# A retention-plus-hard-swish kernel: W_in loaded in eight equal pieces, six short zero matmuls at the begin, one load of the sixth GEMM2 issued later

## The chip, the cores and the metric

One core of a Trainium2 chip runs the whole program. The metric is device time in microseconds of one execution. The kernel before took 286.35 us, the median of three runs (286.25 to 286.49). Engines in the profile: PE (TensorE matmul), PEld (its weight load), DVE (VectorE), ACT (ScalarE), POOL (GpSimd, which issues nearly all loads here), SP (SyncE, which issues stores and transposing DMAs).

## The reference

Two stages, one after the other, on fp32 inputs:

```python
# q, k, v: (8 batches, 8 heads, 576 positions, 64)
scores = q @ k.T / sqrt(64)
ret    = scores * D            # D[i, j] = gamma_h ** (i - j) for i >= j, else 0
x      = (ret @ v)             # heads side by side: (4608 tokens, 512)
h      = x @ w_in              # (4608, 2048)
g      = h * clip(h + 3, 0, 6) / 6
out    = g @ w_out             # (4608, 512), float32
```

## The kernel before

The attention is computed in pieces of 128 positions. A piece turns its own scores against the lower triangle and adds what a running 64 x 64 state per head carries over from the pieces before (linear attention in chunks). The pieces of eight batches are taken in the order of position, so that four pieces fill one block of 512 tokens; there are nine blocks. The 64 positions that are left in each batch form four "rest" pieces, numbers 32 to 35, and the last block.

For each block, GEMM1 multiplies the block's x (512 channels, transposed) with W_in in 16 units of four matmuls of 512 columns (line 478); ACT and DVE make the hard-swish from the PSUM result (lines 486 and 487). GEMM2 multiplies the 2048 features with W_out. For the first two blocks this is 64 plain matmuls of 512 columns (line 541). From the third block on it is `g2_seven`: seven half-size products in the manner of Strassen, 14 units of eight matmuls of 256 columns (line 627), with sums of the weights and of the tokens made ahead on DVE. PE goes through the blocks in a fixed order written out by hand: GEMM1 of a block, GEMM2 of it, GEMM1 of the next. Between units, lists such as `steps_at`, `load_in_gemm2` and `load_in_gemm1` put in the other work: attention steps on PE (`step4`, lines 389, 411, 439 and 357: 128 matmuls of 64 x 64 in all), multiplications and transposing DMAs of the coming piece (`ahead`), and loads (`load_next`).

How the work around the change is ordered:

- **Start.** Batches come in pairs. The first pairs' q, k and v are loaded by `first_load`, converted to fp16, turned by PE (line 262), and give the first block's x. While the first data is on its way, PE multiplies zeros (`warm`, line 226). Weights are then loaded by POOL in the order of lines 690 to 702: W_in in six pieces, three quarters of W_out, pair 2 of q, k, v, the last quarter of W_out, pair 3.
- **First GEMM1.** It begins with three pairs of half-block products (line 506) from the first columns of W_in, and goes on in units of 128 columns: f = 4, 5, ... to 15. W_in's first four loads cover 256 of the 2048 columns each (f = 0,1; 2,3; 4,5; 6,7), the last two 512 each (f = 8 to 11; 12 to 15).
- **POOL's queue.** POOL issues DMAs in program order, and a DMA waits until the eighth one before it has landed, since there are eight semaphores for them.
- **Later loads.** `load_next` issues one third of a piece (k, then q, then v), after the newest matmul that PE has been given at that place in the lists (`newest[0]`, line 759). A rest piece's third is two DMAs.

```python
load_in_gemm2 = {kb: ... (0, 2, 4, 6, 8, 10, 12) ...}    # after which units a third is loaded
load_in_gemm2[5] = (0, 2, 4, 6, 11, 12, 13)              # block 5: the sixth GEMM2
```

Of the kernel before, what the change touches and what calls it, by code (L numbers as in the profile page):

```python
# [10 lines left out]
FP32 = mybir.dt.float32  # L11
# [6 lines left out]
def kernel(  # L18
# [16 lines left out]
    nc = tc.nc  # L35
# [3 lines left out]
    P = 128  # L39
# [4 lines left out]
    MBLK = 512  # L44
# [39 lines left out]
    def bank(shape, dtype, name):  # L84
        return psum.tile(shape, dtype, tag="ph", bufs=4, name=name)

    def bank_or(tag, shape, dtype, name):
        return psum.tile(shape, dtype, tag=tag, name=name) if tag else bank(shape, dtype, name)
# [40 lines left out]
    def load_win(f0, f1):  # L129
        return nc.gpsimd.dma_start(  # L130
            win16[:, :, f0:f1],
            moe_w_in.rearrange("(cc p) f -> p cc f", p=P)[:, :, f0:f1])
# [16 lines left out]
    zeros = const.tile([P, MBLK // 2], FP32)  # L149
# [69 lines left out]
    warmed = [0]  # L219

    def warm(n, tag=None):

        w = bank_or(tag, [P, 2, MBLK // 2], FP32, f"warm_{warmed[0]}")
        warmed[0] += 1
        for _ in range(n):
            nc.tensor.matmul(w, zeros[:, 0:P], zeros[:, None, :].to_broadcast([P, 2, MBLK // 2]),
                             start=True, stop=True)

    warm(3)

    def make_mask64():
        nc.vector.tensor_copy(mask64[0:HALF], mask01[0:HALF, 0:HALF])
# [455 lines left out]


    WQ = DFF // 4  # L690
    for i in range(4):
        load_win(i * (WQ // 2), (i + 1) * (WQ // 2))
    for i in range(2, 4):
        load_win(i * WQ, i * WQ + WQ)
    for i in range(3):
        load_wout(4 * i, 4 * i + 4)
    first_load(2, 0)
# [171 lines left out]
    for kb in range(1, NMB - 1):  # L869
        for at in {1: ((6, 6), (13, 13)), NMB - 2: ((6, 9),)}.get(kb, ((1, 3), (9, 11))):  # L870
            if groups[2:]:
                put_step(kb, at, groups[0], groups[1])
            else:
# [5 lines left out]
    load_in_gemm2 = {kb: (0, 2, 5, 7, 10, 12) if kb == 2  # L879
                     else (0, 2, 4, 8, 9, 11, 13) if kb == 3 else (0, 2, 4, 6, 8, 10, 12)  # L880
                     for kb in range(2, NMB - 3)}
    load_in_gemm2[1] = (2, 4, 8, 9, 12, 14)
    load_in_gemm2[5] = (0, 2, 4, 6, 11, 12, 13)
    load_in_gemm1 = {kb: (0, 2, 4, 7, 10, 13) for kb in range(2, NMB - 2)}
    load_in_gemm1[2] = (0, 1, 2, 4, 7, 10, 13)
    for kb in range(1, NMB):
# [52 lines left out]
```

## Time and profile before

| What | us |
|---|---|
| median of 3 runs | 286.35 |
| profiled execution, its own time | 285.78 |
| span of the profiled execution | 284.0 |
| PE busy | 275.5 (97%) |
| DVE busy | 229.2 (81%) |
| ACT busy | 171.2 (60%) |
| first GEMM1's units of 512 columns, first matmul | 18.05 |
| first GEMM2, first matmul | 28.9 |
| sixth GEMM2 | 182.4 to 197.4 |

The profiled execution lasts 1.78 us longer than its span and is 0.57 us below the median. The span is cut into busy time by engine; since PE is busy for 97% of it, the few places where PE has nothing to run are what is looked for. "idle before <-" names what ended an engine's idle time. A wait "<-issue" is one for which the profile shows no semaphore. The profile's DMA section splits the transfers by queue: "software_dynamic" holds what POOL issues, "hardware_dynamic" what SP and ACT issue, and "instruction" the engines' own programs, which are fetched by DMA too. A matmul's recorded time is longer than its distance from the next, since matmuls overlap: 512 columns are recorded with 379 ns and follow each other every 216 ns, 256 columns with 273 ns and every 109 ns.

### The profile page before, as it was taken

The page shows a single profiled execution, that of the slowest core. Times are in us where ns is not written, and L with a number is a line of the kernel's source. Part 1 is how long each engine was busy: PE and PEld are TensorE (multiplying, and loading weights), DVE is VectorE, ACT ScalarE, POOL GpSimd, SP SyncE. Part 2 cuts the span into 40 slices and gives each one's busy share as a digit, 9 for nine tenths or more (in the row PEclk, how much of TensorE's full clock was granted, in tenths as well). Part 3 has the DMA queues.
Part 4 walks back from the last instruction along what each step waited for, and adds up shares of the span by engine and source line. Part 5 has one row for each costly group of instructions (what it writes and reads, how often), then busy time and mean ns, then how long its engine had stood idle before and what let it go on. Part 6 is the DMA issues. An engine that isn't in the chain of part 4 may idle for free.

```text
span 284.0 us, 9017 instructions
## 1 busy us (share of the span) xinstructions
PE 275.5 (97%) x3824; PEld 180.0 (63%) x3824; DVE 229.2 (81%) x389; ACT 171.2 (60%) x296; POOL 103.2 (36%) x134
## 2 busy tenths in 40 slices
PE   7899999999999999999999999999999999999994
PEld 2564456875474786478646874597459745874583
DVE  6766765998889998999789978998899588727871
ACT  7778316872477637863676558755865487357710
POOL 8942578253353234324333344353750000000000
PEclk9999999999999999999999999999999999999999
DMA  9999999999999999997999999987992250121014
GB/s 136 186 201 206 190 182 178 213 141 142 184 130 160 142 95 151 165 116 77 145 178 125 95 132 167 150 86 111 152 188 50 76 111 0 42 78 36 0 39 111
DMA packets 144008, 35.98 MB, mean 127 GB/s; under 512 B 129728, under 2 KB 142912, under 8 KB 143968
## 3 DMA queue, kind: packets, MB, share of 16 engines
q0 software_dynamic: 104496, 18.23, 84.4%
q1 hardware_dynamic: 38496, 16.52, 29.2%
q10 hardware_dynamic: 976, 0.66, 0.8%
q8 instruction: 30, 0.49, 0.7%
q14 instruction: 10, 0.08, 0.1%
HBM read 36.70 MB, written 9.44 MB: 162 GB/s over the span
## 4 chain that ended last, share of the span: by engine, by line
PE 91%; DMA 4%; POOL 4%; issue 0%; DVE 0%; POOLq 0%
PE ph L478 36%; PE x L627 15%; PE pout L541 10%; PE z L627 9%; PE ph L506 6%; PE y L627 5%; DMA win<-in_moe_w_in_dram 4%; PE o L389 2%; PE o L411 2%; PE sc L357 2%; POOL qkn L121 2%; PE u L439 1%; PE xtu L627 1%; PE xo L627 1%; POOL win L130 1%; POOL vn L121 1%
## 5 line engine op out<-in xcount | busy, mean ns | idle before, releaser
L478 PE MATMUL ph<-xt,win 128*128 128x512 f16 x488 | 107.1, 379 | 0.3 <-DMA win<-in_moe_w_in_dram 0.3
L486 ACT ACTIVATE u<-ph,cb 128x512 f32<-128x512 f32 x122 | 83.5, 687 | 22.1 <-PE ph L478 22.0
L487 DVE SCALAR_TENSOR_TENSOR gt<-u,ph 128x512 f16<-128x512 f32 x122 | 81.2, 684 | 17.1 <-ACT u L486 15.9
L478 PEld LDWEIGHTS <-win 128*128 128x128 f16 x488 | 47.6, 98 | 56.1 <-DMA win<-in_moe_w_in_dram 0.8
L627 PEld LDWEIGHTS <-sum_s 128*128 128x128 f16 x448 | 43.3, 98 | 5.2
L107 POOL DMA_DIRECT2D qkn<-in_k_dram x32 | 26.6, 834 | 39.0 <-PE ph L478 11.0
L107 POOL DMA_DIRECT2D qkn<-in_q_dram x32 | 26.7, 839 | 29.0 <-PE ph L478 9.9
L107 POOL DMA_DIRECT2D vn<-in_v_dram x32 | 26.8, 838 | 26.6 <-PE ph L478 10.1
L627 PEld LDWEIGHTS <-gt 128*128 128x128 f16 x336 | 32.4, 98 | 5.7 <-issue 0.3
L541 PE MATMUL pout<-wout,gt 128*128 128x512 f16 x128 | 29.5, 380 | 0.0
L595 POOL DMA_DIRECT2D out_dram<-osb x1 | 0.6, 625 | 68.2 <-DVE osb L648 68.2
L627 PE MATMUL x<-wsum_t,sum_s 128*128 128x256 f16 x192 | 22.9, 273 | 0.0
L541 PEld LDWEIGHTS <-gt 128*128 128x128 f16 x128 | 11.8, 98 | 13.6
L506 PE MATMUL ph<-xt,win 128*128 128x256 f16 x176 | 20.1, 273 | 0.1
L344 DVE TENSOR_TENSOR qkn<-qkn,gqk 128x1024 f16<-128x1024 f16 x28 | 19.1, 684 | 0.0
L506 PEld LDWEIGHTS <-win 128*128 128x128 f16 x176 | 16.8, 98 | 2.9 <-DMA win<-in_moe_w_in_dram 0.4
L582 DVE TENSOR_TENSOR sum_s<-gt 128x1024 f16<-128x1024 f16 (+1 forms) x21 | 18.1, 863 | 0.2
L514 ACT ACTIVATE u<-ph,cb 128x512 f32<-128x512 f32 x22 | 15.0, 687 | 4.9 <-PE ph L506 4.7
L363 DVE TENSOR_TENSOR at<-sc,mask 128x1024 f16<-128x1024 f32 x14 | 17.0, 1216 | 1.1 <-PE sc L357 1.1
L515 DVE SCALAR_TENSOR_TENSOR gt<-u,ph 128x512 f16<-128x512 f32 x22 | 14.5, 683 | 2.8 <-ACT u L514 2.6
L423 ACT CAST xt<-o 64x512 f16<-64x512 f32 x28 | 16.2, 580 | 0.3
L421 ACT CAST xt<-o 128x512 f16<-128x512 f32 x14 | 8.2, 585 | 10.2 <-PE o L411 10.2
(112 smaller groups left out, 321.5 us busy)
## 6 DMA issues: line engine op xcount, KB each, us to landing
out_dram<-osb SPq DMA_DIRECT2D x24, 256.0 KB, 2.9
qkn<-in_k_dram POOLq DMA_DIRECT2D x32, 128.0 KB, 5.3
vn<-in_v_dram POOLq DMA_DIRECT2D x32, 128.0 KB, 5.0
qkn<-in_q_dram POOLq DMA_DIRECT2D x30, 128.0 KB, 5.3
out_dram<-osb SPq DMA_DIRECT2D x19, 128.0 KB, 5.0
wout<-in_moe_w_out_dram POOLq DMA_DIRECT2D x4, 512.0 KB, 14.9
win<-in_moe_w_in_dram POOLq DMA_DIRECT2D x4, 256.0 KB, 7.3
win<-in_moe_w_in_dram POOLq DMA_DIRECT2D x2, 512.0 KB, 11.4
```

The costliest lines, as they stand in the source:

```text
L107: loaded[c]["dma"].append(nc.gpsimd.dma_start(dst[p0:p0 + n], src[b, :, s0:s0 + n, :].rearrange("h s d -> s h d")))
L344: nc.vector.tensor_tensor(out=both, in0=both, in1=gqk, op=ALU.mult)
L363: nc.vector.tensor_tensor(out=at.rearrange("t a j p s -> t (a j p) s"), in0=sc.rearrange("t a j p s -> t (a j p) s"), in1=mask64[:, None, ...
L423: nc.scalar.copy(to[rows(h2), :, :, 1, :], o[1][rows(1 - h2)].rearrange("e j p s -> e p j s"))
L478: newest[0] = nc.tensor.matmul(ph, win16[:, dmc, P * fc:P * fc + P], xt_of(kb)[:, dmc, :], start=(dmc == 0), stop=(dmc == NCC - 1))
L486: nc.scalar.activation(u, ph, ACTF.Relu, bias=cb[:, 0:1], scale=1.0 / 6.0)
L487: nc.vector.scalar_tensor_tensor(out=gts[kb][:, fc, :], in0=u, scalar=1.0, in1=ph, op0=ALU.min, op1=ALU.mult)
L506: newest[0] = nc.tensor.matmul(ph[:, i], win16[:, dmc, P * (fc + i):P * (fc + i) + P], xt_of(kb)[:, dmc, cols], start=(i == 0 and dmc == 0 ...
L514: nc.scalar.activation(u, ph, ACTF.Relu, bias=cb[:, 0:1], scale=1.0 / 6.0)
L541: newest[0] = nc.tensor.matmul(pout, gt[:, fc, P * mc:P * mc + P], wout16[:, fc, :], start=(fc == 0), stop=(fc == NFC - 1))
L582: nc.vector.tensor_tensor(out=s(which)[:, c0:c1], in0=x(), in1=y(), op=op)
L627: newest[0] = nc.tensor.matmul(dst, left()[:, c, P * u:P * u + P], right[:, c, :], start=(first and c == 0 and (u == 0 or name not in whol ...
```

## The change

Three edits. W_in is loaded in eight pieces of 256 columns; its columns 1024 to 2047 came in two pieces of 512 and come in four. At the begin PE multiplies zeros six times with 256 columns, in place of three times with 512 columns (a view that showed the same 256 zeros twice); each of these fp32 matmuls stands in the trace as two weight loads' and two matmuls' records. In the sixth GEMM2 the fourth load, which is v of rest piece 32, is issued after unit 10 and not after unit 6.

```diff
     def warm(n, tag=None):
-        w = bank_or(tag, [P, 2, MBLK // 2], FP32, f"warm_{warmed[0]}")
+        w = bank_or(tag, [P, MBLK // 2], FP32, f"warm_{warmed[0]}")
         warmed[0] += 1
         for _ in range(n):
-            nc.tensor.matmul(w, zeros[:, 0:P], zeros[:, None, :].to_broadcast([P, 2, MBLK // 2]),
-                             start=True, stop=True)
-
-    warm(3)
+            nc.tensor.matmul(w, zeros[:, 0:P], zeros, start=True, stop=True)
+
+    warm(6)
...
     WQ = DFF // 4
-    for i in range(4):
+    for i in range(8):
         load_win(i * (WQ // 2), (i + 1) * (WQ // 2))
-    for i in range(2, 4):
-        load_win(i * WQ, i * WQ + WQ)
...
-    load_in_gemm2[5] = (0, 2, 4, 6, 11, 12, 13)
+    load_in_gemm2[5] = (0, 2, 4, 10, 11, 12, 13)
```

POOL issues two DMAs more; on every other engine the program's instructions are the same in the same order, apart from the zero matmuls.

## The prediction

> **What bounds the kernel now.** I read the page first: busy time, then the instruction queue.
>
> ```profile
> PE 275.5 (97%) x3824; PEld 180.0 (63%) x3824; DVE 229.2 (81%) x389; ACT 171.2 (60%) x296; POOL 103.2 (36%) x134
> ...
> q8 instruction: 30, 0.49, 0.7%
> ```
>
> PE is the bound, so only PE's idle time can go. PE's own program is also fetched by DMA: 30 packets, 0.49 MB, for 7648 matmuls and weight loads, so 64 bytes each and 256 instructions to a packet. Next the chain that ended last, in order of time:
>
> ```profile
> 8.48 2.89 POOL win L130 x4
> 11.37 10.59 DMA win<-in_moe_w_in_dram
> 22.00 7.08 PE ph L478 x32
> ...
> 135.09 0.67 issue
> ```
>
> The chain reaches PE at 22.00 through the load of W_in's third piece, and from there on it is nearly all PE. The timeline shows the wait, and the zeros at the begin:
>
> ```profile
> 1.19 0.50 PEld L226 LDWEIGHTS warm<-zeros 128*128 128x128 f32 x2 [1.19 <-DVE cb L153]
> 1.19 4.68 PE L226 MATMUL warm<-zeros 128*128 128x512 f32 x6 [1.19 <-DVE cb L153]
> 2.21 0.34 PEld L226 LDWEIGHTS warm<-zeros 128*128 128x128 f32 x1 [0.52 <-issue]
> ...
> 6.75 0.64 PE L262 MATMUL trq<-ident,qkn 128*64 128x128 f16 x16 [0.88 <-ACT qkn L181]
> ...
> 18.05 3.62 PE L478 MATMUL ph<-xt,win 128*128 128x512 f16 x16
> ...
> 22.00 7.08 PE L478 MATMUL ph<-xt,win 128*128 128x512 f16 x32 [0.33 <-DMA win<-in_moe_w_in_dram]
> ```
>
> Sixteen matmuls of 216 ns from 18.05 end their stream at 21.50; the next starts at 22.00. The wait is 0.50 us (the 0.33 is counted from the last one's recorded end). After it PE has no wait for a load. Three more places stop PE for no semaphore:
>
> ```profile
> 71.49 0.23 PEld L411 LDWEIGHTS <-vn 64*64 64x64 f16 x18 [0.16 <-issue]
> ```
> ```profile
> 135.75 0.25 PE L411 MATMUL o<-at,vn 64*64 64x64 f16 x7 [0.67 <-issue]
> ```
> ```profile
> 157.55 0.33 PEld L627 LDWEIGHTS <-gt 128*128 128x128 f16 x4 [0.30 <-issue]
> ```
>
> By the starts of neighbouring matmuls they cost 0.21, 0.83 and 0.19 us: 1.23 together. I counted PE's records: they stand at numbers 1985, 4033 and 4545, each 193 more than a multiple of 256. So PE stands there at the edge of a fetched packet. The packets before them are at 68.64 (1.28 long), 133.50 (0.93) and 154.49 (1.52); PE goes on 1.56, 1.33 and 1.55 after their ends.
>
> **The change, part by part.** *W_in in halves.* The issues and landings:
>
> ```profile
> win<-in_moe_w_in_dram POOLq DMA_DIRECT2D x1, 512.0 KB, 10.6
> win<-in_moe_w_in_dram POOLq DMA_DIRECT2D x1, 256.0 KB, 8.2
> ```
>
> The last 256-column piece was issued at 10.64 and landed at 18.84, the third big one at 21.95, the fourth at 24.24, W_out's quarters at 26.84, 29.36 and 31.87. The queue is full all this time, so bytes and their order set the landings. Two 256-column pieces landed 1.27 and 1.32 after the one before; an instruction packet (at 19.81) falls into the third piece, which took 3.11 where the fourth took 2.29, so up to 0.82 more. The first half then lands between 20.1 and 21.0, and PE wants it at 21.50. The second half lands by about 22.1 and is wanted two units later, at 23.23. Gain: 0.50 us. A loss is bounded by the price of smaller packets: 512-byte packets moved 195 GB/s at 14 to 16 us, 1024-byte ones 205 at 22 to 29 us, so 2 x 0.13 us more for the two pieces. W_out's first quarter then lands at 27.1 and is wanted at 28.42 (28.92 less 0.50), so nothing is lost. Two more issues on POOL (0.83 us each, started every 0.73) go into a queue that has DMAs outstanding for over 10 us. They also move the waits on "the eighth DMA before" by two: the second and third quarters of W_out wait for landings at 16.25 and 17.52 rather than going out at 13.56 and 14.35, still 12 us ahead of their landings, and pair 2's q, k wait for the halves. From pair 2's v on, each DMA waits for the same landing as before. What is late next is W_out's first quarter, with 1.3 us in hand, and nothing else on PE.
>
> *Zeros.* The stream is the same: 12 passes of 256 columns for 6 of 512. It ends about 5.7, and PE is wanted at 6.75, after ACT's cast. Six more weight loads of 0.27 to 0.34 us come beside streams of 0.43. If all were hidden: 0. If none: 6 x 0.34 = 2.0 us, the first transpose 1.0 us later, of which the wait of 0.29 us before 16.29 takes a part. I take 0, since the load at 2.21 begins with the matmul at 2.21 and matmuls follow each other every 0.853 us. The Trainium skill (TensorE: Matmul & The Clock Gate, Part 3, "What overlaps and what doesn't") says that weight loads overlap matmuls in flight only for another row group. By that the six would cost their 2.0 us; the row above, same row group, disagrees.
>
> *Packet edges.* The zeros add 12 PE instructions (six weight loads, six matmuls), so every edge comes 12 instructions earlier in the work. A packet can be asked for when PE's queue passes the edge one packet before; I use the record 64 ahead of it, after which the packets start 1.2 us (at 223) to 5.9 us (at 19.81) later.
> - Edge at 135.75: the asking moves over six 256-column matmuls, 0.66 us earlier; the edge itself lies among 64 x 64 matmuls, 0.05 earlier. 0.83 becomes 0.22: -0.61.
> - Edge at 157.55: asking over 512-column matmuls, 1.3 earlier; need over 256-column ones, 0.65 earlier. -0.19, gone.
> - Edge at 71.49: both among 64 x 64 ones: +0.03.
> - Nearest without a stall: 196.38, also 1.56 after its packet's end (193.78 + 1.04); asking and need both move 0.66: 0. Next nearest: 16.85, 2.06 after; need 0.96 earlier, but a load holds PE until 16.29 there anyway: 0 to +0.15.
>
> Sum -0.77 if packets follow their asking in full. If they don't follow at all, only the needs move: +0.05 + 0.65 + 0.05 + 0.66 = +1.4. Best case: all three gone, -1.23. Packets in quiet stretches (at 214, 223, 248) start 1.2 to 1.3 us after their record, so the first end is nearer; leaving a quarter us for packets that follow in part, I take -0.5.
>
> *The later load.* v of rest piece 32, two DMAs, moves from 190.22 to about 195.0, ahead of k of piece 33 (195.97), which slips to 196.3 at most (2 x 0.68 us of issue). The piece's v is first read by PE at 246.9; piece 33's transposing DMA went out at 209.03 and its q landed at 203.61. SP's stores at 196.57 and 198.06 share the DMA engines with it; their buffers are wanted again at 217. Cost 0, hidden by 50 us of PE's work. It clears the stretch in which the packet of 193.78 is fetched, a gain of 0 there since that edge doesn't stall.
>
> Sum: -0.50 + 0 - 0.5 + 0 = -1.0 us. The profiled execution becomes 285.78 - 1.0 = 284.78; the median is 0.57 above it, so 286.35 - 1.0 = 285.35.
>
> **Rivals.** *Only the load's wait goes.* The packets' stalls change place but not their sum: 286.35 - 0.50 = 285.85, within 0.2% (0.57 us, about what a measurement of this kernel can tell from no change). For it: packets start from 1.2 to 5.9 us after their record, so the asking is not all. The Trainium skill (Runtime: NRT & Kernel Launch, Instruction fetch mechanics) calls crossing a 16 KiB block mostly hidden; by that, moving the edges would change nothing, and the sum would be this one. The trace disagrees at three of 29 edges. The reverse, that the wait at 22.00 stays and the packets gain, gives about the same time.
>
> *A packet comes too late (slower).* Place: the edge at 196.38 (then about 195.7), which has no reserve. Its packet started 2.28 us after its record; the one of 133.50 took 4.05. With that delay it stalls 1.8 us: 286.35 - 0.50 + 1.8 = 287.65 if the other stalls stay. It decides from 1.07 us of added stall on (0.57 + 0.50). Against: loads on the queue are fewer there than at 133, and one is moved away.
>
> *The zeros' weight loads are not hidden:* +1.0 - 0.29 at the first GEMM1, which takes the place of the 0.50 wait: 286.35 + 0.2 = 286.55 with the stalls as before. Against it stands the row at 2.21.
>
> **How the numbers follow.** Forecast, halves and packets both gaining: 0.52, own range 284.6 to 285.75 (all stalls gone: 286.35 - 1.73 = 284.62; packets barely gaining). Only one of the two: 0.20. Packet too late: 0.23. Weight loads: 0.05. Faster by over 0.2% (under 285.78): 0.52. Same: 0.20 + 0.05 = 0.25. Slower (over 286.92): 0.23. The range is 284.6 to 287.1: below it only gains at other edges, above it the larger half of the slow case.
>
> **What the profile after would show.** Right: first GEMM2 matmul at 28.4, no wait for W_in near 21.5; zeros ending near 5.9 and the first transpose at 6.75; PE's "<-issue" waits at records 193 over a multiple of 256 as before, 12 instructions earlier in the work, the one near 135 at 0.2; no wait for v of piece 32. Wrong: a new "<-issue" wait over 1 us, above all near 195; a transpose later than 6.9; a wait for W_out at 28.4.

## The result, and the profile after

The changed kernel takes 284.49 us, median of 9 runs (284.17 to 285.77), against 286.06 us for the kernel before (9 runs, 285.33 to 286.49) beside it. The ratio is 0.9956, with a 95% interval of 0.994 to 0.9972: faster by 0.44%. (It isn't the ratio of the two medians, which lie 1.57 us apart, 0.55%.) The profiled execution took 284.36 us, its span 282.6; before they were 285.78 and 284.0. Forecast were 1.0 us less and a range of 284.6 to 287.1 at a median of 286.35 before; against that median the ratio gives 285.09.

Busy time and the instruction queue, from the page of the kernel after:

```profile
PE 275.0 (97%) x3830; PEld 182.1 (64%) x3830; DVE 229.2 (81%) x389; ACT 171.3 (61%) x296; POOL 104.8 (37%) x136
...
q8 instruction: 30, 0.49, 0.8%
```

PE has six matmuls and six weight loads more, 12 instructions, and PE's busy time is about the same (275.0 us, before 275.5). What PE waited for in the kernel after (in total, times, longest, all in us):

```profile
PE warm L226 <- DVE cb L153: 1.2, 1, 1.2
PE trq L261 <- DVE qkn L703: 0.9, 1, 0.9
PE sc L282 <- ACT tk L266: 0.6, 2, 0.5
PE trk L261 <- ACT tq L266: 0.4, 1, 0.4
```

All of it lies in the first 13 us. There is no line for W_in and none with "<-issue". The timeline after, at the places that the prediction shows of before (the line numbers from there on are one lower now), from four stretches:

```profile
1.20 4.93 PE L226 MATMUL warm<-zeros 128*128 128x256 f32 x12 [1.20 <-DVE cb L153]
...
7.06 0.93 PE L261 MATMUL trq<-ident,qkn 128*64 128x128 f16 x16 [0.93 <-DVE qkn L703]
...
18.11 10.52 PE L477 MATMUL ph<-xt,win 128*128 128x512 f16 x48
...
28.46 3.62 PE L540 MATMUL pout<-wout,gt 128*128 128x512 f16 x16
```
```profile
70.68 0.64 PE L410 MATMUL o<-at,vn 64*64 64x64 f16 x32
```
```profile
134.17 0.46 PE L410 MATMUL o<-at,vn 64*64 64x64 f16 x32
```
```profile
155.00 1.16 PE L626 MATMUL y<-wout,gt 128*128 128x256 f16 x9
```

The first GEMM1's 48 matmuls of 512 columns run in one piece from 18.11, where before they were cut in two at 22.00. The 32 matmuls near 134 run through where they were cut into 25 and 7; the stop near 157 (now near 155) is gone as well. By the starts of neighbouring matmuls 0.1 us is left near 71, and nothing at the two other places. PE's last matmul ends at 278.48, before at 280.06. These 1.58 us are 0.45 up to the first GEMM2, 0.11 near 71, 0.83 near 135 and 0.19 near 157.

So both gains of the forecast seem to be there. Whether they are two, and which edit earns which, only the parts alone can show.

### The profile page after: what moved, and what is told of

Same layout as the page of the kernel before. It is cut to its first block, busy times and chain, and to the rows that moved or that the text cites. A ratio compares the mean times of both kernels' runs of the same rounds, so it can differ in the third digit from the quotient of the medians.

```text
span 282.6 us, 9031 instructions
## 1 busy us (share of the span) xinstructions
PE 275.0 (97%) x3830; PEld 182.1 (64%) x3830; DVE 229.2 (81%) x389; ACT 171.3 (61%) x296; POOL 104.8 (37%) x136
## 4 chain that ended last, share of the span: by engine, by line
PE 94%; DMA 2%; DVE 1%; ACT 1%; issue 1%
PE ph L477 37%; PE x L626 15%; PE pout L540 10%; PE z L626 9%; PE ph L505 7%; PE y L626 5%; DMA plain<-in_q_dram 2%; PE o L388 2%; PE o L410 2%; PE sc L356 2%; PE u L438 1%; PE xtu L626 1%; PE xo L626 1%; PE trq L261 1%; PE sc L282 1%; PE o L308 1%
```

## The experiments

Theory on trial: two separate gains, the wait for W_in (halves) and the edges of the fetched instruction packets (12 instructions more), while the moved load does nothing. Rivals: one edit earns everything; or the shape of the zeros matters and not their number of instructions.

Each kernel's stalls below are read like those in the prediction, from the starts of neighbouring matmuls in its profiled execution; "packet" is the start of the 16 KiB instruction packet that brings the edge in question.

| Kernel | ratio to before, 95% interval | wait near 22 | packet, stall near 71 | packet, stall near 135 | stall near 157 |
|---|---|---|---|---|---|
| before | 1 | 0.50 | 68.64, 0.21 | 133.50, 0.83 | 0.19 |
| e1 halves alone | 1.0004 (0.9991 to 1.0016) | 0 | 68.32, 0.83 | 133.17, 0.82 | 0.46 |
| e2 zeros alone | 0.9945 (0.9927 to 0.9962) | 0.27 | 67.70, 0.09 | 131.01, 0 | 0 |
| e3 after, load as before | 0.9948 (0.9931 to 0.9965) | 0 | 68.88, 0.63 | 130.98, 0 | 0 |
| e4 after, other 12 instructions | 0.9935 (0.9922 to 0.9948) | 0 | 68.34, 0.39 | 130.62, 0 | 0 |
| e5 load alone | 1.0008 (0.9987 to 1.0028) | 0.38 | 68.73, 0.26 | 133.63, 1.11 | 0 |
| after | 0.9956 (0.994 to 0.9972) | 0 | 68.32, 0.10 | 130.44, 0 | 0 |
| e6 after, piece 14 later | 0.9936 (0.9919 to 0.9953) | 0 | 66.92, 0.08 | 130.84, 0 | 0 |
| e7 zeros, piece 14 later | 0.9957 (0.9941 to 0.9973) | 0.46 | 67.24, 0.10 | 130.97, 0 | 0 |
| e8 after, 24 instructions more | 1.0001 (0.9981 to 1.002) | 0 | 67.91, 0.21 | 131.18, 0.09 | 0 |
| e9 halves, piece 14 later | 0.9982 (0.9969 to 0.9994) | 0 | 67.64, 0.07 | 133.03, 1.18 | 0.74 |
| e10 as e9, piece 23 later too | 0.9956 (0.994 to 0.9971) | 0 | 68.19, 0.09 | 132.62, 0.58 | 0.21 |

**e1, the halves alone.**

```diff
-    for i in range(4):
+    for i in range(8):
         load_win(i * (WQ // 2), (i + 1) * (WQ // 2))
-    for i in range(2, 4):
-        load_win(i * WQ, i * WQ + WQ)
```

> Only the first edit: W_in in eight pieces; three zero matmuls and the load as before. Theory (wait for W_in and packet edges are two separate gains): the 0.50 us wait near 21.5 to 22.0 is gone, the three stalls at PE records 193 over a multiple of 256 stay with about 0.2, 0.8 and 0.2 us, and the time falls by about 0.5 us (ratio 0.998). Rival 1 (the halves earn everything, and the stalls went because PE runs 0.5 us earlier against the loads): no stalls, and a fall of about 1.3 us (0.9956). Rival 2 (the wait was hidden anyway): no fall.

Measured: 286.56 against 286.17 us, ratio 1.0004 (0.9991 to 1.0016): no fall. Yet the wait near 22 is gone; the first GEMM2 starts at 27.97 (28.91 before). Of these 0.94 us, 0.44 were there ahead of the halves' place: the units of 512 columns start at 17.61 (18.05 before), and over the profiled executions of all kernels this start lies anywhere from 17.61 to 18.72. PE's waits for no semaphore in this kernel's timeline, three stretches:

```profile
71.16 0.34 PE L411 MATMUL o<-at,vn 64*64 64x64 f16 x18 [0.66 <-issue]
```
```profile
135.40 0.25 PE L411 MATMUL o<-at,vn 64*64 64x64 f16 x7 [0.66 <-issue]
```
```profile
157.47 0.33 PEld L627 LDWEIGHTS <-gt 128*128 128x128 f16 x4 [0.58 <-issue]
```

PE comes to the edge near 71 about 0.95 us earlier than before and goes on only 0.33 us earlier (71.16, before 71.49), as its packet starts at 68.32 (before 68.64). What was left passes the edge near 135 (135.40, before 135.75) and goes at the one near 157 (157.47, before 157.55), where the stall grows from 0.19 to 0.46; PE ends at 279.99 (280.06). The theory fails: the stalls did not stay as they were. Rival 1 falls too, since they did not go. Rival 2 has the right number for the wrong reason: the wait was not hidden, its gain was given back downstream.

**e2, the zeros alone.**

```diff
-    warm(3)      # 512 columns, a broadcast view of 256 zeros
+    warm(6)      # 256 columns
```

> Only the second edit: six zero matmuls of 256 columns; W_in's pieces and the load as before. Theory: the wait near 22 stays at about 0.5 us; every packet edge stands 12 instructions earlier in the work, the stalls near 135 and 157 shrink to under 0.25 us together, and the time falls by 0.8 to 1.1 us (0.996 to 0.997). Rival (the zeros do nothing, the halves or the moved load do): no fall, stalls as before.

Measured: 284.63 against 286.17 us, ratio 0.9945. No "<-issue" line is left among PE's waits, and at the places near 135 and 157 PE runs through:

```profile
134.35 0.46 PE L410 MATMUL o<-at,vn 64*64 64x64 f16 x32
```
```profile
155.18 1.05 PE L626 MATMUL y<-wout,gt 128*128 128x256 f16 x8
```

The wait for W_in near 22 is there, at 0.27 us by the starts. The fall is more than forecast, and as large as the whole change's: by the times, the halves add nothing in the changed kernel that these intervals can tell (0.9956 with them, 0.9945 without).

**e3, the changed kernel without the moved load.**

```diff
-    load_in_gemm2[5] = (0, 2, 4, 10, 11, 12, 13)
+    load_in_gemm2[5] = (0, 2, 4, 6, 11, 12, 13)
```

> The changed kernel with the third edit undone: the load of v of piece 32 again after unit 6. Theory (the load costs and earns nothing): as the changed kernel, ratio 0.9956 to before, no stall over 0.2 us near 195. Rival (the moved load clears the stretch in which a packet is fetched for the edge near 194): a stall of 0.3 to 1 us near 194 to 196, and that much longer.

Measured: 284.86 us, ratio 0.9948; the largest stop from 193 to 197 is 0.11 us. The rival falls. In this execution PE stood 0.63 us near 71, with the halves in place; e2 without them had 0.09 there, and the two ratios are the same.

**e4, 12 other instructions.** The zeros are as before (three of 512), and behind them stand small matmuls:

```diff
     warm(3)
+    w = bank_or(None, [P, MBLK // 2], FP32, "pad")
+    for _ in range(6):
+        nc.tensor.matmul(w[:, 0:8], ident16, ident16[:, 0:8], start=True, stop=True)
```

> The changed kernel with the zeros as before (three of 512 columns), and behind them six small fp16 matmuls of 8 columns, 12 PE instructions, in PE's idle time before 6.75. The edges of the packets then stand where the changed kernel has them. Theory (only the number of instructions matters): as the changed kernel, ratio about 0.9956, no stall near 135 and 157. Rival (the shape of the zeros matters, for instance through the clock): the stalls of before are back, ratio about 0.998.

Measured: 284.46 us, ratio 0.9935, no stop near 135 and 157. So the shape of the zeros isn't needed for it: 12 instructions of another kind ahead of the edges do the same.

**e5, the moved load alone.**

> Only the third edit: v of piece 32 after unit 10 of the sixth GEMM2. Theory (it costs and earns nothing): ratio 1.000 to before, the stalls near 71, 135 and 157 as before. Rival (half of the gain is the load's): a fall of 0.3 us or more.

Measured: 285.99 against 286.03 us, ratio 1.0008 (0.9987 to 1.0028), stops near 71 and 135 as before (0.26, 1.11), none near 157 in this execution. It earns and costs nothing that can be told.

**e6 and e7, the loads ahead of the packet for the edge near 71.** In all kernels so far that packet starts at 67.7 to 68.9, though PE passes the edge before at 64.2 to 66.3. e6 takes two loads out of its way, with the halves; e7 does so without them (zeros alone; e7 lacks the moved load too, which in e5 does nothing that can be told).

```diff
-    for j in (0, 2, 3, 5, 7, 8):                        # second GEMM1
+    for j in (0, 2, 3, 5):
...
-    load_in_gemm2[1] = (2, 4, 8, 9, 12, 14)
+    load_in_gemm2[1] = (1, 2, 4, 6, 8, 9, 12, 14)
```

> The changed kernel with two thirds of piece 14 loaded later: not after units 7 and 8 of the second GEMM1 (62 to 63 us) but after units 1 and 2 of the second GEMM2 (about 66), and the thirds behind them one place later. Theory (the packet for the edge near 71 starts at 67.7 to 68.9 in all kernels since loads issued at 62 to 63 stand before it in the DMA engines, so PE stops there until about 70.9 and whatever was gained before is given back): the packet starts at 66 to 67, no stall near 71, PE ends 0.2 to 0.6 us earlier than in the changed kernel. Rival (the packet's start hangs on PE, not on the loads): start and time as in the changed kernel.

> The second edit alone (six zero matmuls, W_in's last two pieces whole, the load as before) with the same later loads of piece 14. Theory (halves earn 0.3 to 0.5 us where no stall near 71 gives it back): 0.3 to 0.5 us longer than the run with the halves and the later loads, with the wait near 21.7 of 0.3 to 0.5 us. Rival (halves earn nothing): the same time as that run.

Measured: e6 284.27 us (284.19 to 284.55), e7 284.94 us (284.3 to 285.12), on one chip. POOL's loads in the timeline of the kernel after, and of e6:

```profile
62.30 0.87 POOL L107 DMA_DIRECT2D qkn<-in_k_dram  x1 [1.16 <-PE u L326]
...
63.36 0.87 POOL L107 DMA_DIRECT2D qkn<-in_q_dram  x1 [0.19 <-issue]
...
66.71 0.87 POOL L107 DMA_DIRECT2D vn<-in_v_dram  x1 [2.48 <-PE pout L540]
```
```profile
66.11 0.88 POOL L107 DMA_DIRECT2D qkn<-in_k_dram  x1 [5.00 <-PE pout L540]
...
66.97 0.88 POOL L107 DMA_DIRECT2D qkn<-in_q_dram  x1
```

and the instruction queue in e6's window from 66 to 67 (packets, MB, share), where before the packet falls into the window from 68 to 69:

```profile
q8 instruction: 1, 0.02, 6.1%
```
```profile
q8 instruction: 1, 0.02, 8.0%
```

With no load issued between 60.2 and 66.1, the packet starts 1.4 us earlier (66.92, after: 68.32) while PE passes the edge before at the same time (64.48 and 64.51). So loads issued ahead of it delay its start. Four pairs of profiled executions differ in these loads alone (after and e6, e2 and e7, e1 and e9, and the two repeats below): without them the packet comes 0.6 to 1.4 us sooner after its asking in each. What holds it in e6 from its asking, near 64.1, to 66.92 isn't shown. With that stop out of the way the halves earn what was forecast. e7's timeline, then e6's:

```profile
21.88 4.49 PE L477 MATMUL ph<-xt,win 128*128 128x512 f16 x20 [0.30 <-DMA win<-in_moe_w_in_dram]
```
```profile
18.07 8.15 PE L477 MATMUL ph<-xt,win 128*128 128x512 f16 x37
```

The wait is 0.46 us by the starts, PE ends 0.50 us apart (278.92 and 278.42), the medians 0.67.

**e8, twenty-four instructions more.** The changed kernel, with twelve of e4's small matmuls behind the six zeros.

> The changed kernel with 24 PE instructions more (twelve small fp16 matmuls of 8 columns in PE's idle time before 6.75), so that every edge comes 24 instructions earlier still. Theory (edges alone decide; the first packet, asked for near 9 us, arrives near 16.0): a new stall of 0.8 to 1.3 us at the edge that now falls near 14.8 us, of which the wait for W_in near 16 takes a part, none near 135 and 157, and 0 to 0.9 us longer than the changed kernel, since the stop near 71 can take the delay. Rival (instructions at the begin do not matter by number): no stall near 14.8.

Measured: 285.96 us, with a wide spread (285.05 to 287.79); ratio 1.0001. The whole gain is gone, as it can be if the number of instructions at the begin matters. But the place was wrong: the first packet started at 11.73 (13.89 after) and not at the time that I had assumed, and nothing stalls at 14.8. The profiled execution was this kernel's fastest, 285.05, with four stops of about 0.2 us from 71 to 109, of which two (70.7 and 108.9) stand at packet edges; its PE ends 0.70 us later than after's. Where the slower executions lose up to 2.7 us more isn't shown, and with it the cause of the loss stays open.

**e9 and e10, the halves alone, with packets let through.** e9 is e1 with e6's later loads. e10 also moves the loads ahead of the packet for the edge near 135. In both PE runs the same instructions as before.

```diff
-    ... (0, 2, 4, 8, 9, 11, 13) if kb == 3
+    ... (0, 2, 8, 9, 10, 11, 13) if kb == 3             # e10
```

> The first edit alone (halves; zeros and the load as before), with the thirds of piece 14 loaded later as in the run with later loads. Theory (the halves' gain was given back at the edge near 71): no stall near 71, so 0.5 us of the wait for W_in and 0.2 us of the stall are kept until 130; the stalls near 135 (0.8) and 157 (0.2 to 0.5) stay: 0.4 to 0.7 us under the kernel before, ratio 0.9975 to 0.9985. Rival (the halves cost as much as they earn elsewhere): ratio 1.000.

> As the run before this one in the list, and v of piece 23 and the two thirds behind it issued later in the fourth GEMM2 (after units 8, 9, 10 in place of 4, 8, 9), so that no load is issued from 129 to 132 us, when the packet for the edge near 135 is asked for. No PE instruction differs from the kernel before. Theory (a packet that is asked for behind loads comes late, wherever the edge stands): that packet starts near 131 to 132 and not 133.5, the stall near 135 falls from 0.8 to under 0.3 us, and the time falls by another 0.5 to 0.8 us, ratio near 0.9955. Rival (the place of the edge alone decides): the stall near 135 stays.

Measured: e9 285.83 and e10 285.34 against 286.39 us; ratios 0.9982 (0.9969 to 0.9994) and 0.9956 (0.994 to 0.9971). PE's waits in e9, then in e10:

```profile
PE o L411 <- issue: 1.0, 1, 1.0
...
PE y L627 <- issue: 0.6, 1, 0.6
```
```profile
PE o L411 <- issue: 0.4, 1, 0.4
```

In e9 the stop near 71 is gone and PE comes to its third GEMM2 at 94.17 (94.78 before), but it stands 1.18 and 0.74 us at the two later edges, where it stood 0.83 and 0.19: what came through the first is given back at the next, and PE ends at 280.34 (280.06 before). That is one execution, at 286.15 us slower than e9's median. By the times 0.5 us is kept, as the theory had it; why the profile shows none of it kept is open. In e10 the packet for the second starts 3.09 us after the record 64 ahead of its asking (e9: 4.20), and the stop falls to 0.58, not to under 0.3. So packets can be let through by moving loads, with no edge moved; the size was less than expected there, and its profiled execution came 0.7 us later than e9's to the first GEMM2 (29.08, 28.40), after waits for loads of v and W_in, so its profile understates it.

**The changed kernel and e6 side by side.**

> The changed kernel once more, on the chip of the other runs of this list: 284.4 to 284.9 us, ratio near 0.995. It is there to be compared with them.

> The changed kernel with the later loads of piece 14, once more, beside the changed kernel on one chip. Theory (the stall near 71 costs the changed kernel 0 to 0.4 us, by execution): 0.1 to 0.4 us under the changed kernel, and a smaller spread. Rival: no difference.

Measured on one chip: the changed kernel 284.91 us (284.47 to 285.75), ratio 0.9946 (0.9929 to 0.9963); with the later loads 284.46 (284.09 to 284.71), ratio 0.9929 (0.9914 to 0.9943). The medians are 0.45 us apart, the spread is half as wide, but the intervals overlap; and in the two profiled executions, both 284.7 us, neither stops near 71. The later loads give the lowest ratio of the study, by a step that the intervals don't separate: on another chip they had 0.9936, and e4, without them, has 0.9935.

## Why the prediction was right or wrong

The sum was right in sign and nearly in size: 1.0 us were forecast, and the ratio says 1.26 (0.8 to 1.7). Its terms were not: the halves alone earned nothing where 0.50 was forecast, the zeros alone 1.6 us (0.9945) where 0.5 was. That the two errors nearly cancel is luck.

- *Halves, -0.50.* The wait was read rightly, and it went. The step that failed is "What is late next is W_out's first quarter, with 1.3 us in hand, and nothing else on PE". Late next was the instruction packet for the edge near 71, which loads issued ahead of it delay. In e1 the earlier PE only stands longer there. Alone the halves earn nothing (1.0004); behind a packet that is let through they earn 0.50 us of PE's time (e6 against e7), and 0.5 us of the time without the zeros (e9, 0.9982). In the changed kernel they count where the stop near 71 doesn't take them, and that differs from execution to execution: 0.10 to 0.63 us in after, e3 and e4. The landings were read well: the first half landed at 20.25, the second at 22.04 and W_out's first quarter at 26.81, where 20.1 to 21.0, 22.1 and 27.1 were forecast. The price of smaller packets was too low, as the trace has 190 and not 195 GB/s at 14 to 16 us.
- *Zeros, 0 for their time.* Right. The last of twelve passes begins at 5.75, and PE's first transpose follows at 6.57 to 7.06 in the kernels with this form, after a conversion of q. The 7.06 of the kernel after is later than the 6.9 that was named as a sign of being wrong; it isn't the zeros' doing, since e9, with the zeros of before, has 6.95. The Trainium skill (TensorE: Matmul & The Clock Gate, Part 3, "What overlaps and what doesn't") lets weight loads overlap only for another row group; here a load of 0.33 us begins 2 ns after a matmul of the same row group, and from 1.78 to 5.20 us passes follow each other every 0.427 us, the stream's own 0.853 halved.
- *Packet edges, -0.5 out of -0.77.* The mechanism was right, the size was not: 1.23 us of stops before, 0.1 after, and 0.9945 for the zeros alone. The term leaned on packets that follow their asking at most one for one. Near 157 that held: the packet came 2.78 us earlier (151.71, before 154.49), 1.4 of it PE itself being earlier and 1.3 the forecast asking. Near 135 it didn't: the packet came 3.06 us earlier (130.44, before 133.50), of which 0.5 is PE itself and 0.66 the asking, and 1.9 are left over. That an earlier asking can get ahead of a load was not in the sum. Loads can hold a packet up (e6 and e10, where only loads were moved); for the edge near 135 the traces name one, shown below this list. The forecast's near miss came too: the edge that stood at 16.85 now stops PE near 16, for 0.2 to 0.5 us in six of the eight profiled executions with the 12 instructions. The wait for W_in's second piece covers it in three of them and leaves 0.16 to 0.25 us in the others (forecast: 0 to +0.15).
- *Later load, 0.* Right (1.0008 alone, 0.9948 without it).
- *Rivals.* "Only the load's wait goes" had it upside down: the packets gained and the load's wait alone brought nothing. The late packet near 195 didn't come: the packet started at 191.24 and PE passed the edge at 194.14 without a stop. The Trainium skill (Runtime: NRT & Kernel Launch, Instruction fetch mechanics) calls a crossing mostly hidden; here most are hidden indeed, but three of 29 are not, and their stops are 1.2 us in the kernel before and 1.13 of the 1.58 us by which PE ends earlier in the kernel after.

The load for the edge near 135, v of a piece, stands in the timeline before and then after like this:

```profile
129.80 0.87 POOL L107 DMA_DIRECT2D vn<-in_v_dram  x1 [0.86 <-PE x L627]
```
```profile
129.28 0.87 POOL L107 DMA_DIRECT2D vn<-in_v_dram  x1 [0.87 <-PE x L626]
```

Take as the asking, as the prediction does, the record 64 ahead of the edge one packet before. This load is issued 0.35 us behind the asking in before, e1, e5 and e9, and their packets start 4.05 to 4.20 us after the asking. In the eight profiled executions with the 12 instructions (after, e2 to e4, e6, e7 and the two repeats) it is issued 1.01 us behind, and the packets start 2.16 to 2.87 us after. But without this load (e10) it is still 3.09 us, so the load can be only a part of the difference; the rest is open.

## What to carry to other kernels

A stop with no semaphore can be an instruction fetch: count the records between such stops before explaining them by data. Here they stood whole multiples of 256 apart, each with an instruction packet ending 1.2 to 1.6 us before. In a program whose instructions are streamed while the DMA engines are full, a few instructions more or less at the begin move every later edge, as 12 did here, so a comparison of two versions can measure that and not the edit; an edit should also be tried with the number of instructions held, by padding. And a gain ahead of an edge that waits for its packet can be given back there, as in e1: look at the next stop downstream, whatever releases it.

## What the runs showed of the hardware that was not expected

- An instruction packet of 16 KiB takes 0.9 to 1.5 us in most cases (2.2 at most), but starts 1.0 to 7.5 us after the record 64 ahead of the edge before, and PE goes on 1.2 to 1.6 us after its last byte where it waits. Loads issued before it are part of this: with none issued for 6 us it came 1.4 us earlier (e6).
- Twelve PE instructions, none of them on the critical path, are worth 0.55% (e2) to 0.65% (e4, with the halves and the moved load) of the whole time. With 24 more the gain is gone (e8).
